# Block powers and their exponentials laid out channel by channel, in a spectral mixing kernel with an S4 convolution

## The chip, the cores and the metric

The kernel runs on 1 core of one Trainium2 chip. The metric is device time in microseconds (us) of one execution. Executions of one kernel mostly agree within about 1%, but chips differ: the kernel before had a median of 1421 us on one chip and 1445 us on another. So every version is compared with runs of the kernel before on the same chip in the same rounds. Single looks have no state (unknown), and only their traces are used for more than a rough time.

Engines: PE is TensorE (PEld its weight loads), DVE is VectorE, ACT is ScalarE, POOL is GpSimd.

## The reference, cut to what matters

The whole program is a forward pass with its gradients. The change touches only the stage that makes the convolution kernel of the S4 half, here called the kernel loop:

```python
logdA = exp(log_dt)[:, None] * (A_re + 1j * A_im)     # D=1024 channels x N=128 states
P = jnp.exp(logdA[:, :, None] * l[None, None, :])     # lags l = 0..2047
K = jnp.einsum("dn,dnl,dn->dl", Cc, P, dB).real
```

No lag gets its own exponential. A lag is split into a multiple of 8 below 256 (32 of them) plus an offset from a table of 21, and a power is the product of two tables. Table AN holds the 32 block powers of each channel and state, table wO the 21 offset powers with the weights in them. A matmul over the states (128 partitions) joins them.

## The kernel before

States sit on the partitions, N = P = 128. For a block of 128 channels `bi`, with channel d = 32 q + c and power a (0 to 31):

```python
def exps_a(pr_, EA, ps=range(Q32)):          # EA[P, 32, 256]: power, channel; 256 channels = 2 blocks
    for p_ in ps:
        chain(nc.scalar.activation(out=EA[:, p_, :], in_=zr[:, pr_ * 256:(pr_ + 1) * 256], func=ACT.Exp, scale=8.0 * p_))

def unit(dst, E, tab, d0, na, nd):           # sines, then times the exponentials
    ...                                      # ts = phi x tab on DVE, as integers
    chain(sin_of(dst[:, 1], ts[:, 0:F]))
    ...                                      # tq = ts + 16384 on DVE
    chain(sin_of(dst[:, 0], tq[:, 0:F]))
    d4 = dst.rearrange("p c (a d) -> p c a d", d=nd)
    nc.vector.tensor_tensor(out=d4, in0=d4, in1=E.unsqueeze(1).to_broadcast([P, 2, na, nd]), op=ALU.mult)

def sin_a(bi, q, AN, EA):                    # AN[P, 2, 128, 32]: (q, a), then c
    c0 = (bi % 2) * P + 32 * q
    unit(AN[:, :, 32 * q:32 * q + 32, :].rearrange("p c a d -> p c (a d)"), EA[:, :, c0:c0 + 32], p8r[:], bi * P + 32 * q, 32, 32)

def chunk(bi, ch, AN, wO, Kq):               # 4 chunks of 8 channel groups
    ...
    nc.tensor.transpose(trp[:, comp, cc, :], AN[:, comp, :, c], ident[:, :])
    nc.tensor.matmul(pK[:, c4, cc * 4 * NA:(cc + 1) * 4 * NA], lhsT=AN[:, comp, :, c],
                     rhs=wO[:, comp, :, c::32].rearrange("p a q -> p q a"), start=(comp == 0), stop=(comp == 1), skip_group_check=True)
    ...                                      # trp copied out by DVE and ACT in turn
    for q in range(4):                       # pK copied out by ACT
        qs = slice(32 * q, 32 * q + 32)
        nc.scalar.activation(out=Kq[qs, :, ch * 8:ch * 8 + 8].rearrange("p a (k c) -> p a k c", k=2), in_=pK..., func=ACT.Copy)
```

Two things to see. The stationary operand `AN[:, comp, :, c]` takes one bf16 value every 64 bytes. So does, less visibly, the moving operand: `wO[:, comp, :, c::32]`, with the offsets inside, takes one value every 256 bytes. `chain` fixes the order of activations on ACT, so that tables of functions are not reloaded; the 32 exponentials of EA run as a burst, once for each pair of blocks.

## Time and profile before

| | before |
|---|---|
| time | 1421.18 us median of 3 runs (1414.63 to 1425.28) |
| busy in the whole | DVE 80%, PE 76%, ACT 59% of 1424.5 us |
| kernel loop, 472 to 850 us | PE 268, DVE 303, ACT 267 of 378 us, granted clock 0.68 |

The groups of instructions that the change touches, from the list of groups with shapes kept apart (line, engine, operation, tiles, shapes, count | busy us, mean ns of one | idle us of the engine before them and who ended it):

```profile
L903 PE MATMUL pK<-wO,AN 128*128 128x84 bf16 x512 | 99.9, 343 | 3.7 <-DVE st L1013 2.3 <-ACT Kq L913 1.2 <-DVE AN L415 0.2
L903 PEld LDWEIGHTS <-AN 128*128 128x128 bf16 x512 | 75.6, 151 | 10.4 <-issue 5.2 <-DVE AN L415 0.7
L902 PE MATMUL trp<-ident,AN 128*128 128x128 bf16 x512 | 75.1, 277 | 12.5 <-DVE A L907 6.2 <-DVE AN L415 3.9 <-ACT A L909 1.8
L902 PEld LDWEIGHTS <-AN 128*128 128x128 bf16 x512 | 60.9, 158 | 21.4 <-issue 14.2 <-DVE AN L415 4.8
...
L403 ACT ACTIVATE EA<-zr 128x256 bf16<-128x256 f32 x128 | 40.7, 405 | 0.0
L415 DVE TENSOR_TENSOR AN<-AN,EA 128x2048 bf16<-128x2048 bf16 x32 | 40.2, 1257 | 2.9 <-ACT AN L123 2.8
...
L1008 PE MATMUL pK<-xg,S1f 128*128 128x512 bf16 x80 | 35.3, 538 | 44.2 <-ACT Kq L913 35.5 <-DVE st L1013 8.6
```

Durations of PE and ACT instructions overlap those of their neighbours, so a mean duration is not a pace. The pace is the time from one start to the next, worked out from the start times in the trace for instructions that follow each other without idle time. In the loop (median; full and half are the two states of the granted clock that the traces show, 1.0 and 0.5):

| start to start, ns | before, full | before, half |
|---|---|---|
| transpose after transpose (line 902, strided weights) | 64 | 107 |
| transpose after transpose (line 857, contiguous weights) | 56 | 107 |
| pK matmul after pK matmul (line 903) | 165 | 165 |
| exponential of EA after another (line 403), mostly | 306 | |

Busy time by stage, from the windows view (engine, busy us, instructions; then clock, DMA share, GB/s), for the stage before the loop, the loop and the rest:

```profile
290.00:472.00 182.00, 144.55 (x777) 79.21 (x775) 138.80 (x247) 100.69 (x136) 61.46 (x93) 0.95 0.52 127
472.00:850.00 378.00, 268.24 (x1877) 205.89 (x1876) 302.74 (x414) 266.71 (x477) 41.26 (x47) 0.68 0.44 154
850.00:1424.00 574.00, 461.62 (x3469) 338.38 (x3468) 487.30 (x810) 328.28 (x485) 104.36 (x146) 0.89 0.73 193
```

The columns are PE, PEld, DVE, ACT and POOL. In the loop no engine is full, and ACT has 111 us to spare. The timeline of ACT's first burst in the loop, and the first matmul that waits behind it (start us, length us, engine, line, what; in brackets the idle time before it and who ended it):

```profile
519.98 10.00 ACT L403 ACTIVATE EA<-zr 128x256 bf16<-128x256 f32 x32
...
530.00 1.28 ACT L123 ACT_TABLE_LOAD   x1
...
533.39 0.60 ACT L913 ACTIVATE Kq<-pK 32x168 bf16<-32x168 f32 x2
...
535.85 1.01 PE L1008 MATMUL pK<-xg,S1f 128*128 128x512 bf16 x2 [8.85 <-ACT Kq L913]
```

The copies of pK stand behind the burst in ACT's queue, so PE stands idle for 8.85 us until they free the buffer. (Of these, about 3 us fall in the burst; the rest is the table load, the sines and the copies that follow it.) The Trainium skill ("Perfetto Trace Analysis", Tensor Engine Instruction) says that ACT takes its instructions strictly in order, while PE may pull weight loads ahead; this trace agrees: the pK matmuls of the chunk end at 519.48 us and their copies start at 533.39, and a weight load of line 1008 starts at 526.69, while the transposes before it still run (until 527.00) and 9 us before its own matmuls.

### The profile page before, as it was taken

What the parts mean: (1) busy time and instruction counts of PE and PEld (TensorE: products, weight loads), DVE (VectorE), ACT (ScalarE), POOL (GpSimd) and SP (SyncE); (2) the same over time, 40 slices, a digit from 0 to 9 for tenths busy, and PEclk for the clock granted to TensorE, in tenths of its full rate; (3) what the DMA queues carried; (4) which work ended last, traced back from release to release, by engine and by line L of the source; (5) the groups of instructions that cost most, each with busy time, mean ns of one, the idle gap of its engine ahead of it and who ended that gap; (6) DMA issues with size and microseconds to landing.
All of it is one profiled execution on the core that took longest, in us unless ns stands there. A gap on an engine that the chain in (4) does not pass through costs nothing. (4 is left out here: it accounts for less than half of the span.)

```text
span 1424.5 us, 20171 instructions
## 1 busy us (share of the span) xinstructions
PE 1083.0 (76%) x7187; PEld 738.5 (52%) x7187; DVE 1143.1 (80%) x1897; ACT 837.9 (59%) x1277; POOL 243.1 (17%) x489
## 2 busy tenths in 40 slices
PE   2967988677878757656965979688898886779974
PEld 1434544344444554545753756466666654566752
DVE  5568888578569788687878887389999999879997
ACT  2563445584347785786687454356666564768750
POOL 5101110002129311110100010401203032122110
PEclk9769999999999757755866959999999998799986
DMA  3445556147552743334442647889879773888741
GB/s 140 148 146 157 164 159 222 68 131 158 104 97 103 292 163 119 133 121 161 177 146 68 212 140 262 271 128 183 206 143 263 73 230 54 265 305 277 248 162 30
DMA packets 153081, 236.06 MB, mean 166 GB/s; under 512 B 26386, under 2 KB 100754, under 8 KB 149780
## 3 DMA queue, kind: packets, MB, share of 16 engines
q1 hardware_dynamic: 133780, 184.95, 45.7%
q0 software_dynamic: 12960, 48.25, 10.9%
q10 hardware_dynamic: 6240, 1.57, 0.5%
q8 instruction: 56, 0.92, 0.3%
q14 instruction: 45, 0.37, 0.1%
HBM read 126.80 MB, written 107.66 MB: 165 GB/s over the span
## 5 line engine op out<-in xcount | busy, mean ns | idle before, releaser
L1093 ACT ACTIVATE Vt<-f 128x1024 bf16<-128x1024 f32 (+1 forms) x72 | 64.6, 930 | 89.9 <-PE f L1182 52.0
L903 PE MATMUL pK<-wO,AN 128*128 128x84 bf16 x512 | 99.9, 343 | 3.7 <-DVE st L1013 2.3
L1462 DVE TENSOR_TENSOR pd<-Tsb,ORJ 128x5376 bf16<-128x5376 bf16 x32 | 94.1, 2949 | 7.2 <-PE pr L1468 4.4
L1349 ACT ACTIVATE Tsb<-pT 128x704 bf16<-128x704 f32 x112 | 76.6, 755 | 27.0 <-PE pT L1343 26.8
L1191 PE MATMUL pq<-TKT,PY 128*128 128x321 bf16 x544 | 85.5, 304 | 0.8 <-DVE PY L1161 0.6
L902 PE MATMUL trp<-ident,AN 128*128 128x128 bf16 x512 | 75.1, 277 | 12.5 <-DVE A L907 6.2
L1468 PE MATMUL pr<-pd,ident 128*128 128x256 bf16 x504 | 73.2, 299 | 14.8 <-DVE pd L1462 14.7
L583 PE MATMUL p<-TD,UV 128*128 128x512 bf16 x256 | 69.8, 400 | 18.2 <-DVE Y L587 10.5
L903 PEld LDWEIGHTS <-AN 128*128 128x128 bf16 x512 | 75.6, 151 | 10.4 <-issue 5.2
L1093 ACT ACTIVATE XG<-f 128x1024 bf16<-128x1024 f32 (+1 forms) x72 | 68.2, 983 | 21.7 <-PE f L1131 9.2
L940 PE MATMUL kx<-UV 128*128 128x256 bf16 x408 | 73.4, 292 | 2.0 <-DVE spk L948 1.3
L1218 PE MATMUL f<-Vr,S1i 128*128 128x256 bf16 x256 | 69.3, 390 | 6.6 <-DVE Vr L1099 6.6
L902 PEld LDWEIGHTS <-AN 128*128 128x128 bf16 x512 | 60.9, 158 | 21.4 <-issue 14.2
L525 PE MATMUL p<-DP,UV 128*128 128x512 bf16 x256 | 64.4, 392 | 9.7 <-ACT UO L529 9.2
L1013 DVE CAST st<-pK 128x1024 bf16<-128x1024 f32 x40 | 48.7, 1219 | 26.0 <-PE pK L1008 25.8
L1008 PE MATMUL pK<-xg,S1f 128*128 128x512 bf16 x80 | 35.3, 538 | 44.2 <-ACT Kq L913 35.5
L663 PE MATMUL p2i<-T,Z 128*128 128x512 bf16 x224 | 60.0, 389 | 10.3 <-ACT UV L674 5.3
L1343 PEld LDWEIGHTS <-A2t 128*128 128x128 bf16 x512 | 46.7, 104 | 40.2 <-issue 23.9
L1191 PEld LDWEIGHTS <-PY 128*128 128x128 bf16 x544 | 53.5, 99 | 26.0 <-DVE PY L1161 1.6
L1468 PEld LDWEIGHTS <-ident 128*128 128x128 bf16 x504 | 52.5, 107 | 27.2 <-DVE pd L1462 14.2
L1343 PE MATMUL pT<-BD,A2t 128*128 128x176 bf16 x448 | 51.9, 249 | 16.4 <-DMA A2t<-at 9.6
L1148 DVE TENSOR_TENSOR m<-XG,kb 128x1024 bf16<-128x1024 bf16 (+1 forms) x80 | 46.8, 606 | 16.5 <-ACT XG L1093 11.8
(843 smaller groups left out, 3292.5 us busy)
## 6 DMA issues: line engine op xcount, KB each, us to landing
at<-A SPq DMA_DIRECT2D x32, 512.0 KB, 2.7
st<-st SPq DMA_DIRECT2D x64, 256.0 KB, 6.0
A2t<-at SPq DMA_DIRECT2D x32, 512.0 KB, 7.3
Sg<-st SPq DMA_DIRECT2D x24, 512.0 KB, 12.1
on_scr<-OP SPq DMA_DIRECT2D x8, 1344.0 KB, 4.8
ORJ<-on_scr POOLq DMA_DIRECT2D x8, 1344.0 KB, 8.6
spk<-spk SPq DMA_DIRECT2D x64, 128.0 KB, 1.8
kb<-spk SPq DMA_DIRECT2D x32, 256.0 KB, 4.1
```

The lines of the kernel that those rows point to most:

```text
L525: nc.tensor.matmul(pd[:, eo, :], lhsT=V[:, eo * 2 + c_, b_, :, :].rearrange("p k n -> p (k n)")[:, h::H16], rhs=DP[:, eo * 2 + c_, b_, :], ...
L583: nc.tensor.matmul(ps[:, eo, :], lhsT=U[:, dc, (eo * K16 + k1r) * P:(eo * K16 + k1r + 1) * P], rhs=TD[:, dc, eo, :], start=(dc == 0), stop ...
L902: nc.tensor.transpose(trp[:, comp, cc, :], AN[:, comp, :, c], ident[:, :])
L903: nc.tensor.matmul(pK[:, c4, cc * 4 * NA:(cc + 1) * 4 * NA], lhsT=AN[:, comp, :, c], rhs=wO[:, comp, :, c::32].rearrange("p a q -> p q a") ...
L940: nc.tensor.matmul(px[:, comp, :], lhsT=TK[ci][:, k1, comp, :], rhs=Kc[:, ci, :], start=(ci == 0), stop=(ci == 4 and comp == 1))
L1093: nc.scalar.activation(out=out, in_=in_, func=ACT.Copy)
L1191: nc.tensor.matmul(pq[:, half, 0:NLG // 2], lhsT=PY[:, k_, comp, 256:384], rhs=TKT[:, p0 + k_, comp, half * (NLG // 2):(half + 1) * (NLG / ...
L1218: nc.tensor.matmul(py[:, hh, :, :], lhsT=S1i[:, f_, :], rhs=Vr[:, :, 2 * (hq * HQ + hh) + f_, :], start=False, stop=(f_ == 1), skip_group_ ...
L1343: nc.tensor.matmul(pT[:, cc, 0:4 * NX], lhsT=A2[:, comp, cl * N:(cl + 1) * N], rhs=BD[:, c0_ + cc, :, :].rearrange("p q x -> p (q x)"), st ...
L1349: nc.scalar.activation(out=to_, in_=ti_, func=ACT.Copy)
L1462: TT(out=pd[:], in0=Tsb[:, k_].rearrange("p (g a) d -> p g a d", g=2)[:, :, 0:NA, :], in1=O_.unsqueeze(1).to_broadcast([P, 2, NA, P]), op= ...
L1468: nc.tensor.matmul(pr[:], lhsT=idt[:], rhs=pd[:, :, a_, :], start=(k_ == 0 and a_ == 0), stop=(k_ == 1 and a_ == NA - 1))
```

## The change

The intent: AN is laid out as [component, channel group c, 128 powers], so that the 128 weights of a load are neighbours. To keep the product AN x EA contiguous, EA is laid out channel by channel too. The diff, cut to its core:

```diff
 def new_ea():
-    return kps[0].tile([P, Q32, 256], dt.bfloat16, name="EA")
+    return kps[0].tile([P, 256, Q32], dt.bfloat16, name="EA")
 def exps_a(pr_, EA, ps=range(Q32)):
     for p_ in ps:
-        chain(nc.scalar.activation(out=EA[:, p_, :], in_=zr[...], func=ACT.Exp, scale=8.0 * p_))
+        chain(nc.scalar.activation(out=EA[:, :, p_], in_=zr[...], func=ACT.Exp, scale=8.0 * p_))
 def sin_a(bi, q, AN, EA):
-    unit(AN[:, :, 32 * q:32 * q + 32, :]..., EA[:, :, c0:c0 + 32], p8r[:], bi * P + 32 * q, 32, 32)
+    dst = AN[:, :, :, 32 * q:32 * q + 32]
+    ...                        # ts = phi x p8r, now (channel, power)
+    chain(sin_of(dst[:, 1], ts[:], 32))
+    ...                        # tq = ts + 16384
+    chain(sin_of(dst[:, 0], tq[:], 32))
+    nc.vector.tensor_tensor(out=dst, in0=dst, in1=EA[:, c0:c0 + 32, :].unsqueeze(1).to_broadcast([P, 2, 32, 32]), op=ALU.mult)
-    nc.tensor.transpose(trp[:, comp, cc, :], AN[:, comp, :, c], ident[:, :])
-    nc.tensor.matmul(pK[...], lhsT=AN[:, comp, :, c],
+    nc.tensor.transpose(trp[:, comp, cc, :], AN[:, comp, c, :], ident[:, :])
+    nc.tensor.matmul(pK[...], lhsT=AN[:, comp, c, :],
                      rhs=wO[:, comp, :, c::32].rearrange("p a q -> p q a"), ...)     # not changed
-    return kw.tile([P, 2, P, 32], dt.bfloat16, name="AN")
+    return kw.tile([P, 2, 32, P], dt.bfloat16, name="AN")
```

The number and the order of instructions stay the same on every engine. An exponential now writes one bf16 value every 64 bytes.

More of the change, by code (lines that the diff above doesn't have):

```diff
@@ L120, in low16, with sin_of @@
         return ap.bitcast(dt.uint16)
-    def sin_of(dst, ti_flat):
-        return nc.scalar.activation(out=dst, in_=low16(ti_flat)[:, 0::2], func=ACT.Sin, scale=-TWO_PI / 65536.0, bias=pi_b[:])
+    def sin_of(dst, ti_flat, inner=0):
+        src = low16(ti_flat)[:, 0::2]
+        if inner:
+            src = src.rearrange("p (a b) -> p a b", b=inner)
+        return nc.scalar.activation(out=dst, in_=src, func=ACT.Sin, scale=-TWO_PI / 65536.0, bias=pi_b[:])
     pctx = ExitStack()
@@ L398, in new_ea, with ti_tile @@
     def new_ea():
-        return kps[0].tile([P, Q32, 256], dt.bfloat16, name="EA")
+        return kps[0].tile([P, 256, Q32], dt.bfloat16, name="EA")
     def exps_a(pr_, EA, ps=range(Q32)):
         for p_ in ps:
-            chain(nc.scalar.activation(out=EA[:, p_, :], in_=zr[:, pr_ * 256:(pr_ + 1) * 256], func=ACT.Exp, scale=8.0 * p_))
+            chain(nc.scalar.activation(out=EA[:, :, p_], in_=zr[:, pr_ * 256:(pr_ + 1) * 256], func=ACT.Exp, scale=8.0 * p_))
+    def ti_tile():
+        return kps[0].tile([P, 1024], dt.int32, name="ti_", bufs=2)
     def unit(dst, E, tab, d0, na, nd):
@@ L842, in sin_a @@
                 c0 = (bi % 2) * P + 32 * q
-                unit(AN[:, :, 32 * q:32 * q + 32, :].rearrange("p c a d -> p c (a d)"), EA[:, :, c0:c0 + 32], p8r[:], bi * P + 32 * q, 32, 32)
+                d0 = bi * P + 32 * q
+                dst = AN[:, :, :, 32 * q:32 * q + 32]
+                sq = [P, 32, 32]
+                ts = ti_tile()
+                nc.vector.tensor_tensor(out=ts[:].rearrange("p (d a) -> p d a", a=32), in0=phi[:, d0:d0 + 32].unsqueeze(2).to_broadcast(sq),
+                                        in1=p8r[:].unsqueeze(1).to_broadcast(sq), op=ALU.mult)
+                chain(sin_of(dst[:, 1], ts[:], 32))
+                tq = ti_tile()
+                nc.vector.tensor_single_scalar(out=tq[:], in_=ts[:], scalar=16384, op=ALU.add)
+                chain(sin_of(dst[:, 0], tq[:], 32))
+                nc.vector.tensor_tensor(out=dst, in0=dst, in1=EA[:, c0:c0 + 32, :].unsqueeze(1).to_broadcast([P, 2, 32, 32]), op=ALU.mult)
             ones_k = kc.tile([1, P], dt.bfloat16, name="ones_k")
@@ L901, in chunk @@
                         for comp in range(2):
-                            nc.tensor.transpose(trp[:, comp, cc, :], AN[:, comp, :, c], ident[:, :])
-                            nc.tensor.matmul(pK[:, c4, cc * 4 * NA:(cc + 1) * 4 * NA], lhsT=AN[:, comp, :, c],
+                            nc.tensor.transpose(trp[:, comp, cc, :], AN[:, comp, c, :], ident[:, :])
+                            nc.tensor.matmul(pK[:, c4, cc * 4 * NA:(cc + 1) * 4 * NA], lhsT=AN[:, comp, c, :],
                                              rhs=wO[:, comp, :, c::32].rearrange("p a q -> p q a"), start=(comp == 0), stop=(comp == 1), skip_group_check=True)
```

## The prediction

> **What bounds the kernel now.** The page: DVE 80% busy, PE 76%, ACT 59% of 1424.5 us; none limits throughout. The change touches the kernel loop, 472 to 850 us. There (busy time by window) PE is busy 268 of 378 us, DVE 303, ACT 267, at a granted clock of 0.63 to 0.75. Waits: ACT's copy of the transposes for PE 34 us, PE's `pK` buffer for ACT's `Kq` copies 35 us.
>
> **What the change does.** Instruction counts and order stay the same on every engine (built and compared); only access patterns change.
>
> 1. 1024 weight loads of AN (lines 902, 903) read neighbours instead of one value per 64 bytes. A load takes 148 to 166 ns now; contiguous ones in the loop (line 940, full clock) 98 ns. But loads overlap matmuls, so I read start-to-start times. Transposes (902), with strided loads, follow each other at 107 ns at half clock, as contiguous ones (857) do, and at 64 against 56 ns at full clock: the strided load is nearly hidden. pK matmuls (903, 84 columns) follow at 165 ns at either clock. I put this mostly on their moving operand `wO`, which stays strided: line 1218, strided moving operand but contiguous weights, takes about 200 ns for 128 separate pairs, 1.6 ns each; 84 x 1.6 to 1.7 is 134 to 143. About 22 of the 165 may be the strided load's. Estimate: 340 x 22 + 60 x 25 (902-903 pairs at full clock) + 110 x 8 = 10 us less PE time, half of it on the path: -5 us. The Trainium skill ("TensorE: Matmul & The Clock Gate", Weight-path perf modes) says fast weight load reads its chunks packed or strided, so I expect no change of mode; the 56 to 64 ns agree.
>
> 2. 128 exponentials of EA (line 403, 405 ns, 306 start to start) now write single bf16 values 64 bytes apart. One hint: line 860 writes bf16 with gaps of one value and takes 876 ns for 640, where line 909's rate would give 707: 0.25 ns more per value. Estimate: 256 x 0.25 = 65 ns each, 8 us of ACT, 6 us in the three bursts of 32 in the loop (from 520, 626, 742 us) where PE waits on ACT. On the path: +3 us. The Trainium skill ("SBUF — State Buffer", cachelines) warns of accesses that cross to a new 16-byte line each time; for ACT writes no run here shows it yet.
>
> 3. Sines into AN (1.14 us) and the product AN x EA (1.22 us) work in runs of 32, the phase product (1.21 us) swaps its broadcasts: unchanged within 3%.
>
> **Prediction.** 1421 - 5 + 3 - 1 (loads exposed at starts of bursts) = about 1418 us; 8 in 10 between 1402 and 1432. Faster by over 2% 0.07, within 2% 0.88, slower 0.05.
>
> **What would show it.** AN weight loads 98 to 110 ns at full clock; transposes 56 ns apart at full clock, 107 at half; pK matmuls 140 to 145 ns apart, not under 130; EA exponentials 330 to 400 apart; AN product 1.2 us; PE's busy time in the loop lower by about 10 us, the loop by under 8.
>
> **What would make it wrong.** pK matmuls paced by the load after all: they fall to about 80 ns, 40 us of PE, 20 us of time. Strided ACT writes costing double: 25 us of ACT, mostly before waiting PE, slower by 10 us.

## The result, and the profile after

| | before | after |
|---|---|---|
| time, median | 1421.96 us (4 runs) | 1517.51 us (4 runs, 1515.9 to 1522.09) |
| ratio | | 1.0685, 95% interval 1.0637 to 1.0733: slower |
| first transpose of the loop starts at | 472.7 us | 493.7 us |
| loop, first transpose to last pK matmul | 375.9 us | 443.0 us |
| from there to the end | 575.9 us | 579.5 us |

A ratio here is the mean time of one kernel's fast runs over that of the other's of the same rounds, so not quite the ratio of the medians. The three lower rows come from the two traces: of 92 us, 21 are lost before the loop, 67 in it, 4 after it. (The expectation of run 7 counts from the first weight load, 0.4 us earlier.)

The same groups after:

```profile
L406 ACT ACTIVATE EA<-zr 128x256 bf16<-128x256 f32 x128 | 145.7, 1592 | 0.0
...
L919 PE MATMUL pK<-wO,AN 128*128 128x84 bf16 x512 | 90.2, 321 | 4.1 <-DVE st L1029 2.2 <-ACT Kq L929 1.7 <-DVE AN L859 0.2
L918 PE MATMUL trp<-ident,AN 128*128 128x128 bf16 x512 | 71.6, 275 | 14.1 <-DVE A L923 7.2 <-DVE AN L859 3.9 <-ACT A L925 2.3
L919 PEld LDWEIGHTS <-AN 128*128 128x128 bf16 x512 | 60.1, 119 | 16.5 <-issue 5.5 <-DVE AN L859 0.7
L918 PEld LDWEIGHTS <-AN 128*128 128x128 bf16 x512 | 53.4, 128 | 24.2 <-issue 17.1 <-DVE AN L859 4.8
L859 DVE TENSOR_TENSOR AN<-AN,EA 128x2048 bf16<-128x2048 bf16 x32 | 39.5, 1235 | 2.6 <-ACT AN L126 2.5
L1024 PE MATMUL pK<-xg,S1f 128*128 128x512 bf16 x80 | 35.4, 540 | 97.1 <-ACT Kq L929 88.6 <-DVE st L1029 8.5
```

The loads are shorter, as intended, the pK matmuls too, and the product is as it was. The exponentials take 1592 ns where they took 405. PE's wait for ACT's `Kq` copies, in the last line, went from 35.5 to 88.6 us. The stages after:

```profile
290.00:493.00 203.00, 149.61 (x763) 81.86 (x774) 138.54 (x243) 125.69 (x135) 66.91 (x93) 0.90 0.47 113
493.00:937.00 444.00, 255.20 (x1876) 187.11 (x1874) 300.04 (x413) 342.59 (x473) 37.76 (x47) 0.65 0.37 130
937.00:1516.00 579.00, 459.50 (x3469) 335.41 (x3468) 488.25 (x813) 329.30 (x489) 105.12 (x147) 0.90 0.72 192
```

In the loop PE has 13 us less to do, ACT 76 us more, and the loop is 67 us longer: 76 less about 10. (A few matmul records can be missing from a trace, so PE's busy time is good to a few us.) And the same burst with what stands behind it:

```profile
539.73 35.98 ACT L406 ACTIVATE EA<-zr 128x256 bf16<-128x256 f32 x32
...
575.72 1.28 ACT L126 ACT_TABLE_LOAD   x1
...
578.20 1.23 DVE L853 TENSOR_TENSOR ti__4772<-phi,p8r 128x1024 int32<-128x1024 f32 x1 [27.36 <-ACT AN L126]
579.11 0.59 ACT L929 ACTIVATE Kq<-pK 32x168 bf16<-32x168 f32 x2
...
581.57 1.01 PE L1024 MATMUL pK<-xg,S1f 128*128 128x512 bf16 x2 [34.79 <-ACT Kq L929]
```

The burst is 26 us longer (35.98 against 10.00), and PE's wait behind it is 26 us longer (34.79 against 8.85). DVE, which was hardly waiting there, now waits 27 us for the sines that also stand behind it. Nothing fills the hole.

In starts, inside a burst an exponential follows another after 1110 ns (before: 306), 804 ns more. For 128 of them that is 128 x 0.804 = 103 us of ACT. At the same time the transposes came to 56 ns at full clock and the pK matmuls to 145 ns at both clocks.

### The profile page after: what moved, and what is told of

Same layout as the page of the kernel before. It is cut to its first block, busy times and chain, and to the rows that moved or that the text cites. A ratio compares the mean times of both kernels' runs of the same rounds, so it can differ in the third digit from the quotient of the medians.

```text
span 1516.2 us, 20145 instructions
## 1 busy us (share of the span) xinstructions
PE 1073.7 (71%) x7161; PEld 720.6 (48%) x7187; DVE 1141.9 (75%) x1897; ACT 940.3 (62%) x1277; POOL 245.0 (16%) x489
## 5 line engine op out<-in xcount | busy, mean ns | idle before, releaser
L406 ACT ACTIVATE EA<-zr 128x256 bf16<-128x256 f32 x128 | 145.7, 1592 | 0.0
L1024 PE MATMUL pK<-xg,S1f 128*128 128x512 bf16 x80 | 35.4, 540 | 97.1 <-ACT Kq L929 88.6
L919 PE MATMUL pK<-wO,AN 128*128 128x84 bf16 x512 | 90.2, 321 | 4.1 <-DVE st L1029 2.2
L918 PE MATMUL trp<-ident,AN 128*128 128x128 bf16 x512 | 71.6, 275 | 14.1 <-DVE A L923 7.2
L1484 PE MATMUL pr<-pd,ident 128*128 128x256 bf16 x504 | 68.4, 286 | 15.1 <-DVE pd L1478 14.9
L1024 PEld LDWEIGHTS <-S1f 128*128 128x128 bf16 x128 | 14.0, 114 | 118.7 <-issue 113.4
L919 PEld LDWEIGHTS <-AN 128*128 128x128 bf16 x512 | 60.1, 119 | 16.5 <-issue 5.5
L918 PEld LDWEIGHTS <-AN 128*128 128x128 bf16 x512 | 53.4, 128 | 24.2 <-issue 17.1
```

What stands on the lines that cost most here:

```text
L406: chain(nc.scalar.activation(out=EA[:, :, p_], in_=zr[:, pr_ * 256:(pr_ + 1) * 256], func=ACT.Exp, scale=8.0 * p_))
L918: nc.tensor.transpose(trp[:, comp, cc, :], AN[:, comp, c, :], ident[:, :])
L1484: nc.tensor.matmul(pr[:], lhsT=idt[:], rhs=pd[:, :, a_, :], start=(k_ == 0 and a_ == 0), stop=(k_ == 1 and a_ == NA - 1))
```

## The experiments

The theory after the result: all of the loss is the stores of the exponentials, and the layout of AN itself is a small gain. The rivals: something else in the layout costs time; the 64-byte step is a special, bad step; or the loss belongs to lone stores as such. A fourth question was left from the prediction: what paces the pK matmuls.

### 1. The new layout, with exponentials that store neighbours

```diff
-chain(nc.scalar.activation(out=EA[:, :, p_], in_=zr[...
+chain(nc.scalar.activation(out=EA[:].rearrange("p d a -> p (d a)")[:, p_ * 256:(p_ + 1) * 256], in_=zr[...
```

> The changed kernel with one thing undone: each exponential of EA writes its 256 values next to each other again (wrong result on purpose: the product then reads values of other channels; shapes, counts and order on every engine are those of the changed kernel). Theory (the strided stores of the exponentials cost the whole 92 us, the new AN layout itself saves a little): exponentials back at about 405 ns each, time 1405 to 1421 us, a ratio of 0.99 to 1.00 to the kernel before. Rival (the layout of AN costs time elsewhere: sines or product writing runs of 32, weight loads, a lower granted clock): time stays above 1450 us.

Measured (result wrong): 1421.15 us against 1427.93 us before on the same chip, ratio 0.9958, 95% interval 0.9907 to 1.0009, five rounds. From its list of groups:

```profile
L919 PE MATMUL pK<-wO,AN 128*128 128x84 bf16 x512 | 90.3, 320 | 4.8 <-ACT Kq L929 2.4 <-DVE st L1029 2.2 <-DVE AN L859 0.2
...
L406 ACT ACTIVATE EA<-zr 128x256 bf16<-128x256 f32 x128 | 40.5, 403 | 0.0
```

The loss is gone with the strided stores, and the shorter loads and matmuls stay. What the new layout of AN is worth alone is at most 1% and not clear of zero.

### 2. The old layout, with exponentials that store 64 bytes apart

```diff
-chain(nc.scalar.activation(out=EA[:, p_, :], in_=zr[...
+chain(nc.scalar.activation(out=EA[:].rearrange("p a d -> p (a d)")[:, p_::Q32], in_=zr[...
```

> The kernel before with one thing of the change: each exponential writes its 256 values 64 bytes apart (wrong result on purpose; all else as before, AN in the old layout). Theory: exponentials 1590 to 1640 ns each, and time 1515 to 1535 us, at or a little above the changed kernel, since the weight loads don't get cheaper. Rival: time 1421 to 1450 us.

Measured: 1525.29 us against 1427.93, ratio 1.0711 (1.0641 to 1.0781). Its output is wrong, which doesn't matter for the time. The exponentials:

```profile
L403 ACT ACTIVATE EA<-zr 128x256 bf16<-128x256 f32 x128 | 146.0, 1602 | 0.0
```

With the first experiment this makes a full square: each layout of AN with each way of storing. The stores alone make the loss, with either layout. Between runs 1 and 2 (same chip) the loop differs by 84 us (366.5 and 450.1) and its start by 26 us (467.9 and 493.5); the rest of the program is the same (581 us). An estimate from the paces comes near these 110 us: 103 us of exponentials, and 512 pK matmuls with 20 ns more each, 10 us.

### 3. Rows of EA padded from 64 to 68 bytes

```diff
-    return kps[0].tile([P, 256, Q32], dt.bfloat16, name="EA")
+    return kps[0].tile([P, 256, 34], dt.bfloat16, name="EA")        # the product reads 0:32
```

> The changed kernel with the rows of EA padded from 32 to 34 values, so that the exponentials store 68 bytes apart and not 64 (right result). If the cost comes from a power-of-two step (stores falling on one bank), the exponentials drop below 700 ns and the time comes near 1421 us. If each lone value pays for its own store whatever the step, they stay at 1550 to 1650 ns and the time at about 1517 us.

Measured (right result, one look): 1514.24 us, and the exponentials as dear as before padding:

```profile
L406 ACT ACTIVATE EA<-zr 128x256 bf16<-128x256 f32 x128 | 144.3, 1572 | 0.0
```

So it is not a conflict at a power-of-two step. Against run 1 on the same chip, the loop is 75.4 us longer and starts 21.7 us later: 97 us of time for 128 x 0.79 = 101 us of ACT work (starts 1095 ns apart here). So nearly all of the added ACT time is on the path.

### 4. Stores with other steps

```diff
+w_, s_ = ((fl_b, 1), (fl_b, 2), (fl_b, 4), (fl_b, 8), (fl_b, 16), (fl_b, 31), (fl_f, 16), (fl_f, 4))[p_ // 4]
-chain(nc.scalar.activation(out=EA[:, :, p_], in_=zr[...], func=ACT.Exp, scale=8.0 * p_))
+chain(nc.scalar.activation(out=w_[:, 0:255 * s_ + 1:s_], in_=zr[...], func=ACT.Exp, scale=8.0 * p_ if p_ < 24 else 0.0))
```

Here `fl_b` is EA as one row of bf16 values and `fl_f` the same memory as fp32.

> A measurement, wrong result on purpose: in the changed kernel the 32 exponentials of a burst store with steps of 2, 4, 8, 16, 32 and 62 bytes (bf16, four of each, in this order), then fp32 values 64 bytes and 16 bytes apart; EA is cleared first. Start to start, contiguous is 306 ns. If the cost is that of a 16-byte line that is left with each value: 4 bytes about 370 to 450, 8 bytes 500 to 700, 16 bytes and more all about 1110, fp32 at 64 and 16 bytes also about 1110. If the cost is that of storing two bytes alone (a read and a write of the word): all bf16 steps of 4 bytes and more cost about 1110 and fp32 about 306 at either step. If the cost grows with the step as such: 16 bytes well below 32, and 32 below 62.

The stores of this run overlap, so each exponential waited for the one before it: from 8 bytes on, the next mostly starts about 30 ns after the end, and in the contiguous and 4-byte rows 30 to 350 ns after it. So the paces that the expectation names can't be read; the durations of instructions that run alone can. Medians of 16 each:

| store | duration, ns | added for each value, ns |
|---|---|---|
| bf16 contiguous | 417 | |
| bf16, 4 bytes apart | 488 | 0.28 |
| bf16, 8 bytes apart | 773 | 1.4 |
| bf16, 16 bytes apart | 1336 | 3.6 |
| bf16, 32 bytes apart | 1278 | 3.4 |
| bf16, 62 bytes apart | 1311 | 3.5 |
| fp32, 16 bytes apart | 652 | 0.9 |
| fp32, 64 bytes apart | 628 | 0.8 |

The cost rises until the step is 16 bytes and then no further, so the step as such is not it. An estimate: about 4.35 ns for each 16-byte line (from 1110 ns for 256 lines) fits the bf16 rows: 64 lines at 4 bytes would be 278 ns in place of the 213 ns that 256 values take at 0.83 ns (in the trace before, copies of 1024 values take 1027 ns in line 909 and of 512 values 596 in line 946, 0.84 ns a value); that is 65 added, 71 measured. 128 lines would be 557 ns (344 added, 356 measured), and 256 lines 1114 ns (901 added, 860 to 919 measured). The Trainium skill ("SBUF — State Buffer", the note on SBUF cachelines) has the 16-byte line and says that at least two hits in a line are needed for full bandwidth; here two bf16 values in a line, 8 bytes apart, still cost 1.4 ns more each, and four 0.28, so for these stores two hits are not enough. But fp32 stores cost about a quarter as much, which the line alone does not explain. The next run takes that up.

### 5. Other forms of the store, on ACT and on DVE

```diff
+forms = [lone bf16 x3, pairs x3, fours x3, eights x3, lone fp32 x3]     # all 64 bytes apart, 256 values each, cut
+for d_, s_ in forms:
+    chain(nc.scalar.activation(out=d_, in_=s_, func=ACT.Exp))
+nc.vector.tensor_copy(...)   # two contiguous, two lone bf16, one lone fp32, one of pairs
```

> A measurement on the kernel before (result stays right): ahead of the second set of exponentials, 15 more that store into a spare buffer 64 bytes apart, three of each: lone bf16 values, pairs, fours, eights (256 values each), lone fp32 values; and on DVE, casts of 256 values that store bf16 contiguously (twice), lone bf16 64 bytes apart (twice), lone fp32, and bf16 pairs. If ACT pays for a lone two-byte store and not for the line as such, pairs cost what fp32 costs per store (0.9 ns more per store, about 500 ns in all) and fours and eights about 400 ns. If it pays 3.5 ns more per line touched, pairs take about 860 ns and fours about 620 ns. If the dear store is ACT's own, DVE's lone bf16 casts stay within 100 ns of the contiguous ones; if it is the memory's, they take 1000 ns or more.

Measured (result right, one look). On ACT, start to start in ns: lone bf16 850 (the first) and 1120 to 1130; pairs about 305 (but 605 for the first, behind the lone stores); fours and eights 305; lone fp32 about 445. On DVE, casts of 256 values:

```profile
300.98 0.29 DVE L415 CAST mc<-zr 128x256 bf16<-128x256 f32 x1
...
510.56 0.71 DVE L417 CAST EA<-zr 128x256 bf16<-128x256 f32 x1
...
511.65 0.70 DVE L418 CAST EA<-zr 128x256 bf16<-128x256 f32 x1
511.95 0.74 DVE L419 COPY EA<-zr 128x256 f32<-128x256 f32 x1
512.47 0.35 DVE L420 CAST EA<-zr 128x256 bf16<-128x256 f32 x1
```

In order: contiguous bf16, two of lone bf16, lone fp32, bf16 pairs. On ACT it is the lone two-byte value that is dear: pairs of bf16, in as many lines as half the lone values, cost nothing over contiguous stores. Neither expectation for pairs (500 and 860 ns) was right in size; the first was right in kind. So the line alone is not the cost. An estimate made afterwards fits all forms of runs 4 and 5: about 4.35 ns for a line that takes its bf16 values singly, and 445 / 256 = 1.74 ns for a line that takes whole four-byte words. Pairs would then need 128 x 1.74 = 223 ns, about what their 256 values need anyway (213). No run tested it on a new form. On DVE a lone store costs too, but 1.6 ns more a value (0.71 against 0.29 us for 256, durations of single instructions; no burst of them was measured), and fp32 costs as much as bf16. In durations ACT's lone bf16 values cost 3.4 to 3.6 ns more (run 4), so moving such stores to DVE would, by this estimate, about halve the cost, not remove it. Why ACT pays more for two bytes than for four is not settled by these runs.

### 6. Reading EA across in place of storing it across

```diff
-    return kps[0].tile([P, 256, Q32], dt.bfloat16, name="EA")
+    return kps[0].tile([P, Q32, 256], dt.bfloat16, name="EA")       # exponentials contiguous again
-                                ... in1=EA[:, c0:c0 + 32, :].unsqueeze(1)...
+                                ... in1=EA[:, :, c0:c0 + 32].rearrange("p a d -> p d a").unsqueeze(1)...
```

> A real version, right result: AN in the new layout, EA in the old one (exponentials store neighbours), so that the product AN x EA reads EA 512 bytes apart on DVE. The list scheduler gives it another order, so only durations and the total are compared. If DVE reads lone values as dearly as ACT stores them, the product goes from 1.22 to 4 us or more and the time is above 1460 us; if it only loses the pace of two values a cycle, about 2.2 us and 1425 to 1445 us; if the read is free, 1.22 us and 1410 to 1421 us.

Measured (right result): 1491.55 us against 1445.08, ratio 1.0325 (1.0289 to 1.0362). The product:

```profile
L859 DVE TENSOR_TENSOR AN<-AN,EA 128x2048 bf16<-128x2048 bf16 x32 | 116.4, 3638 | 3.2 <-ACT AN L126 3.1
```

It takes 3638 ns where it took 1257 before and 1235 after (means), 1.78 ns for each of its 2048 values. That is between the first expectation (over 4 us) and the second (2.2 us), nearer the first. (The second takes its factor of two from the trace before: the product has 2048 bf16 values in 1218 ns, the phase product of line 408 1024 four-byte values in 1224.) The disorder has only moved to another engine. The order of instructions also changed in this version, so its total is that of a version, not the price of the read alone.

### 7. Strided stores in the first burst only

```diff
-out=EA[:, :, p_]
+out=EA[:, :, p_] if pr_ == 0 else EA[:].rearrange("p d a -> p (d a)")[:, p_ * 256:(p_ + 1) * 256]
```

> The changed kernel with strided stores in the first 32 exponentials alone (those before the loop), the other 96 storing neighbours; wrong result on purpose. From the two traces, the first transposes start 21 us later in the changed kernel (493.3 against 472.3), the loop lasts 67 us longer and the rest 4 us. If that division is right, this run costs 15 to 25 us over the run with all stores contiguous (about 1435 to 1446 us). If the first 32 are hidden behind the end of the stage before, it equals it (1415 to 1425 us).

Measured: 1460.91 us against 1445.08, ratio 1.012 (1.0071 to 1.0169). Its output is wrong, which doesn't matter for the time. The ratio of run 1 was 0.996, so the first 32 cost 1.6%, about 23 us (the totals named in the expectation were for a faster chip). The trace agrees: the loop is 367.9 us long, as in run 1 (366.5), but starts at 501.1 us, where runs 8 and 9 on the same chip start at 477. The 32 exponentials before the loop are not hidden either: 32 x 0.804 = 26 us of ACT, 23 of them on the path.

### 8. and 9. The other operand of the pK matmul

```diff
-rhs=wO[:, comp, :, c::32].rearrange("p a q -> p q a")
+rhs=wO[:, comp, :, 4 * c:4 * c + 4]
```

On the kernel before (run 8):

> The kernel before with one edit, wrong result on purpose: the pK matmul's moving operand takes runs of four neighbours of wO (columns 4c to 4c+3 of each offset) in place of lone values 256 and 64 bytes apart; the weight loads of AN stay strided. My theory (pK matmuls are paced by their moving operand, with about 22 ns from the strided load): start to start falls from 165 ns to 60 to 110 ns, PE's busy time in the loop falls by 25 to 45 us, total 1395 to 1415 us. Rival (paced by the strided load): start to start stays above 140 ns and the time at 1421 us.

On run 1 (run 9):

> Both edits together, wrong result on purpose: the new AN layout with exponentials that store neighbours (the first experiment), and the moving operand in runs of four. If load and moving operand each set a part of the 165 ns, pK matmuls come to 45 to 85 ns and the total 5 to 10 us under that of the run with the moving operand alone; if the load hides behind the matmul once it is not read against a strided operand, the two totals are equal within 0.3%.

Measured (five rounds, same chip, before 1445.08 us): run 8 1415.09 us, ratio 0.9799 (0.9766 to 0.9832); run 9 1411.39 us, ratio 0.9793 (0.9748 to 0.9838). Their outputs are wrong, which doesn't matter for the times. The matmul and its load in run 8, then in run 9:

```profile
L903 PE MATMUL pK<-wO,AN 128*128 128x84 bf16 x512 | 51.5, 247 | 8.8 <-DVE st L1013 4.3 <-ACT Kq L913 4.3 <-DVE AN L415 0.2
L903 PEld LDWEIGHTS <-AN 128*128 128x128 bf16 x512 | 48.2, 165 | 11.4 <-issue 10.1 <-DVE AN L415 0.7
```

```profile
L919 PE MATMUL pK<-wO,AN 128*128 128x84 bf16 x512 | 42.6, 225 | 9.5 <-DVE st L1029 5.0 <-ACT Kq L929 4.3 <-DVE AN L859 0.2
L919 PEld LDWEIGHTS <-AN 128*128 128x128 bf16 x512 | 36.6, 113 | 12.4 <-issue 10.8 <-DVE AN L859 0.7
```

| pK matmul after pK matmul, ns | full clock | half clock |
|---|---|---|
| before: both strided | 165 | 165 |
| run 1: weights contiguous | 145 | 145 |
| run 8: moving operand in fours | 62 | 71 |
| run 9: both | 38 | 71 |

The moving operand sets most of the pace. Making the weights contiguous took 20 ns off, making the moving operand near took 103 and 94 off, with the load still strided and longer than ever in the records (165 ns). The strided load costs something with either operand: 20 ns at both clocks beside the strided one, and 24 ns at full clock (62 against 38) and nothing at half clock (71) beside the near one. How the two strides add up is not shown. The 38 ns of run 9 is what the Trainium skill ("TensorE: Matmul & The Clock Gate", Back-to-back issue gap) gives at full clock for a matmul of 84 columns, an estimate of 84 / 2.4 + 2.5 = 37.5 ns. The page calls this the gap of an isolated matmul and gives about 81 ns at 128 columns for a stream of pairs of load and matmul; the matmuls here are such pairs and still keep the short gap (the transposes, 128 columns, 56 ns). With the strided operand, the formula is off by a factor of four. And the 24 ns that run 9 has over run 8 are worth nothing that these runs can see in the total: 0.9793 and 0.9799, each to about 0.4%.

### 10. A version that beats both

The kernel before, with the channels of a block in the order c*4 + q in all that leads to wO: phi and the exponents of EO are copied into that order on POOL, the weights are written in it, and the order is undone where the program's last stage copies results out of PSUM, the memory that matmuls write to. AN and EA stay as they were before.

```diff
+zp = peo.tile([P, 256], dt.float32, name="zp")
+nc.gpsimd.tensor_copy(out=zp[:].rearrange("p (b c q) -> p b q c", b=2, q=4), in_=zr[...].rearrange("p (b q c) -> p b q c", b=2, q=4))
...                                   # likewise phi for each block; weights wb on POOL
-rhs=wO[:, comp, :, c::32].rearrange("p a q -> p q a")
+rhs=wO[:, comp, :, 4 * c:4 * c + 4]
-in_=pK[...].rearrange("p k (c q a) -> p a k c q", c=4, q=4)[:, :, :, :, q]
+in_=pK[...].rearrange("p k (c a q) -> p a k c q", c=4, q=4)[:, :, :, :, q]
-to_ = Tsb[:, comp].rearrange("p x (q c) -> p x q c", q=4)[:, :, :, c0_:c0_ + 4]
+to_ = Tsb[:, comp].rearrange("p x (c q) -> p x c q", q=4)[:, :, c0_:c0_ + 4, :]
...                                   # the final copy of pr into res puts the channels back
```

> A version that may beat both, right result: the kernel before with AN and EA as they were, and the moving operand wO put in an order (channel pairs c*4+q inside a block) in which the four columns of one channel group are neighbours. The order comes from permuted copies of phi, of the exponents for EO and of the weights on POOL, and is undone when the transposed results are copied out at the end. Measured with a wrong result, the neighbouring reads alone gave a ratio of 0.980. Expected: pK matmuls 60 to 72 ns start to start, ratio 0.975 to 0.990, against at least 0.995 for the rival that the permuting copies and copies out eat the gain.

Measured (right result): 1403.96 us (1401.07 to 1413.04) against 1428.26 on the same chip, ratio 0.9833 (0.9785 to 0.988). pK matmuls are about 60 ns apart at full clock and 71 at half:

```profile
L907 PE MATMUL pK<-wO,AN 128*128 128x84 bf16 x512 | 50.5, 243 | 8.6 <-DVE st L1017 4.2 <-ACT Kq L917 4.2 <-DVE AN L417 0.2
...
L396 ACT ACTIVATE EO<-zp 128x256 bf16<-128x256 f32 x84 | 26.4, 407 | 0.5 <-POOL zp L394 0.5
```

All of it is 1.7% faster than the kernel before, which is clear of zero, and near the 2.0% of run 8, so the copies on POOL cost little. The loop is 348.3 us long, as in run 8 (348.5). The granted clock in it is 0.75, where the kernel before had 0.68; the runs do not separate how much of the gain comes from that.

## Why the prediction was wrong, point by point

It gave 1418 us with "same" at 0.88. The change is 6.9% slower.

- **The gain in PE (step 1): right in its paces, not shown in its size.** The loads came to 98 ns (transposes) and 115 ns (pK matmuls) at full clock, the second a little over the 98 to 110 that were written; transposes came to 56 and 107 ns and pK matmuls to 145 ns, as written. PE had 13 us less to do in the loop, against "about 10 us". The gain alone was 0.4% or 6 us in run 1, against "-5" and "-1", but this is not clear of zero. That the moving operand sets most of the 165 ns was right as well (runs 8 and 9).
- **The cost of the stores (step 2): this is the step that failed.** The text says "256 x 0.25 = 65 ns each, 8 us of ACT". Measured: 804 ns each from start to start, 103 us of ACT. The 0.25 ns came from line 860, whose values are 4 bytes apart, and it was right for 4 bytes: run 4 shows 0.28. It was carried to 64 bytes, where a line holds one value and not four. The prediction itself named the cachelines page and the crossing of a line each time, and then did not count the lines.
- **The share on the path, also step 2.** It put 3 of 8 us on the path. Measured: about 97 of 101 us (run 3 against run 1). The burst stands in front of the copies that PE waits for and the sines that DVE waits for, on an engine that works in order; that ACT was busy only 71% of the loop made no difference.
- **Step 3: right.** The product had a median of 1219 ns (before 1218), the sines 1.15 us (before 1.15), the phase product 1.22 us (before 1.22).
- **What would make it wrong.** The first alternative, pK matmuls paced by the load, did not come. "Strided ACT writes costing double" named the cause, with 25 us of ACT; the paces show a factor of 3.6. The doubt was there, but it was not made part of the range: 5% for slower was far too little for a cost that no instruction of the trace had shown.

What stays open: why a lone two-byte store costs ACT 4.3 ns and a four-byte one 1.74 ns. That they do is shown; a reason is not. It is not a fixed price for each lone two-byte store, for at 4 bytes apart such a store cost only 0.28 ns more (run 4).

## What to carry to other kernels

A layout change moves the stride from one access to another; price the new stride where it lands, from a measured instruction with the same step and the same width of stored value, and not from a neighbour with a smaller step. A burst on an engine that works in order delays what stands behind it, however idle that engine is on average: here about 97 of 101 us of it were on the path. Before making one operand of a matmul contiguous, see from the start-to-start times which of the two sets the pace: here it was the moving operand, and fixing that one gave 1.7%.

## What the Trainium skill lacked or had wrong

- "ScalarE: Activation LUTs" (step-by-step) gives one value per cycle and lane, 0.833 ns, whatever the function. That holds for contiguous stores (306 ns for 256 values, of which 213 are values by the page's rate, an estimate) and not for lone bf16 stores: 1110 ns for the same 256, 4.3 ns a value. No page has a figure for it.
- "SBUF — State Buffer" (cachelines) names a penalty for crossing a line without a size, and does not tell stores from reads or one engine from another. Measured on ACT, start to start: one lone bf16 value per line 4.3 ns a value, one lone fp32 value 1.74 ns, one bf16 pair nothing over contiguous. On DVE, by duration: lone stores 1.6 ns more a value for bf16 and fp32 alike; a product that reads one of its inputs 512 bytes apart 1.78 ns a value, against about 0.6 contiguous.
- "TensorE: Matmul & The Clock Gate" gives the spacing of matmuls by columns and clock, with or without weight loads, and nothing for the step of the moving operand. With a moving operand of lone values 256 bytes apart, 84 columns took 145 ns (contiguous weights) or 165 ns (strided weights) at either clock, against 38 ns with runs of four and contiguous weights at full clock.
- The same page says that fast weight load reads packed or strided chunks and gives no price for the stride. A transpose's load with a 64-byte step takes 148 ns at full clock against 98 in the records, and such loads hold the pK matmuls to about 62 ns apart against 38 (runs 8 and 9).
